# Seven PSUM banks in one tile, waits per bank, any unit in any bank, and a new order of work

## The chip, the cores and the metric

The kernel runs on one core of a Trainium2 chip. The metric is the device time of one launch in microseconds (us). Five engines work side by side on the core, each through its own queue in program order: TensorE (PE) multiplies matrices into PSUM, VectorE (DVE) and ScalarE (ACT) read PSUM and write SBUF, GpSimd (POOL) works from SBUF to SBUF, and SyncE (SP) issues most of the DMAs. PSUM holds eight banks; one bank takes 128 partitions of 512 float32 values, which is the output of one matmul.

## What is computed

The reference mixes two branches, row by row, with a gate:

```
g = sigmoid((x * gate_w).sum(-1))                 # x: 2048 x 448
a = softmax(q k^T / sqrt(28)) v, 16 heads, @ wo    # q, k, v = x @ wqkv
b = irfft2(rfft2(B_x) * (w_r + 1j w_i))            # 2048 x 448
out = g * a + (1 - g) * b
```

In the data as given `B_x` plays no part: the reference hands `x = A_x` to both branches. All inputs and the output are bfloat16.

## The kernel before

**Tiling of the attention.** The sixteen heads form four groups `g` of four heads `s`; the 2048 queries form four blocks `c` of 512. The sixteen pairs (g, c) are numbered `n` and run one after the other. For each n the 2048 keys are sixteen tiles `kt` of 128. A *unit* (n, kt, s) is one matmul of 32 rows of `k` by 512 columns of `q`; its output is one PSUM bank of 128 keys by 512 queries. The four heads of a tile use four different groups of 32 rows of the PE array, so up to four units can run side by side; PE work of this kind is called *row* work below. The sums over the keys (`pv`, four matmuls of 32 output columns each), the projections and most of the Fourier branch use four groups of 32 columns instead, which is *column* work.

**Two ways to take the exponential.** For most tiles ACT reads two units at once, 128x1024, and writes `exp` into a ring of 28 slots (`ring`, L1034). There are 374 such steps. For 69 tiles, given by `ND` and called d tiles, DVE takes an approximate exponential instead: one `tensor_scalar` a unit (L993) writes 16-bit patterns into `pd`, and three `int64_add` of POOL (L1003) make three shifted copies of them; the four versions are weighted and summed by `pv`.

**The other work.** The Fourier branch (`fwd`, `fwd2`, `mid`, `inv`), the projections of later groups, the normalisation after each n and the output tiles fill the time between. Each piece takes one PSUM bank, named an `Item`, from its first matmul to the DVE or ACT instruction that reads it last.

**PSUM.** `alloc` (L334 to L337) makes separate tiles: `psA` and `psB` with two banks each for the units of ACT, `pvb` with one bank for the sums, and three single banks `bg`. Step i writes `psA` for even i and `psB` for odd i, and so waits for step i-2 of ACT. All else, the units of the d tiles too, goes through the three `bg` banks. The framework derives waits from the tiles that an instruction touches.

**The order.** Nothing is ordered at run time. `Sched.op` collects 3639 operations; `TABLE` holds a list of numbers, found by a search beforehand, in which they are emitted (`Sched.run`), and a list of banks for the Items. Six of the numbers stand for short filler matmuls with zeros (`filler`). Every engine does its share of the list in that order. `step` operations emit both units of a step in one operation.

**The shared port.** `pin` and `ported` make POOL wait for the DVE instructions marked `lk=True`, which work from SBUF to SBUF in 16-bit types, before it goes on to its next instruction.

Of the kernel before, what the change touches and what calls it, by code (L numbers as in the profile page):

```python
# [29 lines left out]
UNITS = 128.0  # L30
# [8 lines left out]
    "eNoN1mNjWEsUQNHxnMG5SW2ltm3bNtPUtm3btm3bto3UdvveX9hf1jakJbHEkXCCJDqJQWKSWCQ2iUPikngkPiEkAUlIEpHEJAkJI0lJMpKc"  # L39
    "UJKCZCApSU6SiniSmuQijHQlQAKiCScZSRoiSXaSlkQlitQk6Ugmkp7UILVINZKNZCG5SVUSheQhWUkOUodkJiVJKRKNlCa1SV5SloSQUFKO"  # L40
    "1Cf5SH5SgBQiBUkxUp6UIRVJYVKEFCXFySZSgWwmlUgJ0oq0JVvIVrKStCPbyHayiqwmVcgOsoZMJGtJZTKJTCZTyFSyjqwnG0g3YpVXG8l0"
    "MoPMJLOIU7PJHDKX7CTziCDzySy/gCwkcWk8Gp8uIovJDL+ELCUJaEK6jKDaRRLRnqQxWU5WkECFqMQ0Ck1Co9JoNDqNQcNoTBqLxqZx6G6y"
    "h+wl+0ioak6iqqfkGXlOXpCXJILcIQ3IfhJJ7pID5B55RV6TKOo+eUMekI7kIXlEHpNo6iCJrqaRGKouOUSS0mQ0pupEYqnkNAU9TJ6Qt2SD"
    "j63ekfckjvpA4qp4qhc5Qo6SlDS+akGOkan0I/lEptHPpAlJoBKq6fQLSaS+Qip6nCRWJ0hqmkR9gxk0TH0lp8hpkoau8WnpGXKWJFX1SG9y"
    "jpwnF8hMepEkU61JOnqJXCZXyFVyjSRX18kNcpOkULfIbZKeplRlaAaakZ4kmWhinoSnUj+hLE2t0qhYvByNzcvTXxCNz/XpVFpVgX6H6Dy9"
    "oqYiHUQyqIzqG0nGm5HvJAaPyX+Qn6Qp+UUyqT+QWf2DSjSLyqo6k+okDk/OK9OGpArtSDvRuDwhX+ezqc60C82uEvD1PhEP439IUp5D/SX/"
    "CKGUMrrac9qV5lSCSqqoprkU0Kw0G81Oc9DcKif9TXLR3NRQS/PQPCovzUdTcEfzKk/z05keaUDj83wqhBagmWlBWogWpkVofpWFhtJ4vCgt"
    "RtuTNqQ47U4LqIw8E+9BS9Ke1PJCyhhtHC+oCqv0vIjiJgMvTaUppoqqtLy4siYlr0p70RKqGi2pqtNSKh0vrVJzYXrTUlSZYaSMKkHT8Bq0"
    "Jk3FmSmrsvFyipi/UF5l5dn5SFpB5eGjaEU1mlZSeXkOPobWopVVB/IbqqiqKhcfS535AdVUTg6mNq2ucvMaqh7tQurTBjQfr0NrKm9qqc+u"
    "MC/DG9J4Bk1dWlsV4XVUDNOI1FUFeEJTkNdTCUwjmpnXV1l4WV6IJzHFeQlegefnFXkDFcs0VDFNXFOTN1KNVWNandfg8U0TVZQnMk1VMhOY"  # L50
# [12 lines left out]
    "6h+om7yaf6j6mt7mPb3C39K7fKCpbx6pW/yxOs3P8idqmhllnqqrfDi5xO/xZ2qcGW/e0RfquXrCL/OyfqIp55/ya3y0eakiVRPfwLxSTf0Y"
    "81rd5s38ZPNGhfs7/AV/q5r7l/ydivAzTDFf3JfwJX0p38K/V/PNB9WflPaRfJB5xT+qT2q2iefL+Bv8DL/OJ5np5rP6ogabIeQRf8af88J+"
    "gvmqvqnH/Av/yhubsaaIf8inmO/qh+JMsE/8p/qlPvOpRjLFNBtK3vJ3/D3/rf6omWaO+av+8n98sVloiP7AP/J/SorlZpYhYoihWgmm+5Hh"
    "huvXfK5ZYRaZN/w3L+qFpuIPlzqnz+V/8G+8oVda6wXmO8/th5lGfpmJKn5y0L+40UvMPPM/SMLqbn6p8drpaMIK1N39SpOE9fA9fS8PLLro"
    "7QO9yYSxpGyECdGhOoZIxvr47aaxj6qFiKKTMycOmW2Gieg6mtYiVHgRQ4OIIraY3SamiCVi6h1mp6nuY+lAxNYJxFGTUMTRIWK/SSJQ1PBx"
    "dZjYZ/aYeDq+TqDjiaEmvqjla/s6vq6v51eZ1SaRSCzq+7giqWjgy/uEerOZ7deYRHqUH+3H+LE+sR7nx/sJfq+ZQE6aOT6JDtNpxFbT0ifV"
    "yXRynVa08W19O9/exxEXTAff0Y80KXRKvc7U9J38QdPKf6Cp9Ef6iaYTqXUanVwcM+nFZ5pWp9OpRGyRXp8xJ8xh84WmFhl0Rl1I7DKFRV/f"
    "z6cQ030ykUmfNwdMZp1FZ9U5RUqRS3T2XXwGsdYcN9l0PnHKZNcD/EA/yGcU+cVgP8Tn0Dl1EXHEFBWnTSaRS2cVQ/1Zk1vHYHl0NnHOxGTD"  # L70
    "fD6dV180XX1mEYtlEbFZft3f3zIFdEEdh2UXf+h685fmEHlEIb3BFNYlxT9aStwx5UURTVgFQVleUVQ/N7lFaXHJFNNTfHE91d8zZcRDU0KX"
    "1DXEffPAlNI1RWldQBQU70w8VkaXFa19OXHbxGfFxHBfVidgI3xCVk1UFIlYdVFOV9Dl9RNTQnyjE/1I/9J8pxV1FVFJ/6A/aRU9yVfWTQVj"
    "03xV8Ys+Mq9NNV1c1Bdf6TNTVTcQv+ld89hU1zV0LVFbTPZPTU0dwmrpSiLSGNZMWPbFvDDzfG093y/wdfRCX1fU0+lZBpaRZWJ1tWOhLAqL"
    "yj6YuOyjWeQvm/o6GsvMGosGuol4axrphnoEaShasEainqgsWrJWrDVrwxKztqwda8+ysSO+sc7OOrAlfqPJwXKyXOyKaaKb6twsD8vLOrJO"
    "rDM75LuwrqwbS8G6s2Z6kz/oo7PNfosP159Nc11H9GBb/Suzzb8xrUSEbqFbi/fmk2mlW+o2Ih9rLvKzr6YAO+ALsraiEIvCC7PWuggryrqK"
    "Nrqt/vf/jKZk10w7vd2318Qu9t1EwIqxVCxceCbsN9NBdxZdRGC9bSc66gixw3fSRz23V/0Vv9S3F501s6lZF91CtBTL/E3fVS/3K7y0g8RK"
    "v8p30zv9Lr/bG5uVdddRbA89WPQUe3xH0VP3EunYft9La7vX7/OdhLLIFrJFrIPoo3vrAWIxW8IGir56Keun++shwtm1bKgAO0BfNWlZP7GO"
    "pWEDdX9h7XgxQQzSg/V6toEN0RtZNDuYXfPdxTA9VN8wQ9hQNlKM0MPEcB3dHvbXzU3TQ4wSw9hwFsOOECP1WDFOXPaj9Gh93Y9ko9gYPVrc"
    "8HFtHzGajWFj9Rjx3YxlP8wtf9vf8Xf9MX/cT9D3/Dg9Xo9nJ/xXN4FNZLFsX9aPDRcn/UQ9iZ3yvcVk1p9F+km6r/jnx7Epeor4Y0awAWwK"
    "m6wHsjg2tg2xy9kKtpKtYoPYVD1Nz9Cv/G8T1aKNaafrqeyBX82ysKliGpupQ208O0vPEMVZCTZTlGSlWGlWhpVl5dhEMVu/8DtZebaLReXL"  # L80
    "WAX208zRFdkmVolVZnP1braHzWB7WRVWlVVj83R1lszOZvf9dDaHLdBr2DQxXcxlr/18PY8t1DNZcruPzRLzGcFFegHLYJfozHax3sxS2GV6"
    "qY5vF4tU9peZLbawBHaJ2MYe+kd+hV4o0trlepGYxR77rWyeWKlX6b/mia/BarKL7BK7zCaLWqw2q8Oe+rrsCqvH6rMGbI3ewZ751bohmyO2"
    "s0Zsrb7KGrNrrAkbTZqy66wZC2fN2Tp9gB1kh9gNFsFuslvsMDvCbrP1+g67yzbo+eIoO8Y26ePsBNuoT7I+bLM+xU6zM6w3u8fOsnPsPLvP"
    "zvgHbIs+7Qval/6X36oXiLP+ITvnz/tterteKi6w7PaNnyso/vbI09kduhdbJlaJ1DaL/et36g1il+7JEtrdOpdNb1eLC/6iv+TXiOd+rdij"
    "U9q8dp8eT1aIjWKd2Kv36/2sgH3r3/n14r3fLg7oD/6gzmQz2t3ijz+kc9jDOredJI7ojz4G7hBbRRq7XETDbSI6bhEMOR7Vm8UecUwLlKgw"
    "nx1Ljuv8NgquFCf0IZHTHhbZ7Cl9Um8Sx8RpndXmscdFIXtR7BS7xBl9Vj9iUfGcLm0vifO6rP3kjwiNKfCCvqgT2fK2kt0vjopL+ry4IB6z"
# [1384 lines left out]
```

## Time and profile before

| | us |
|---|---|
| device time, median of three runs | 380.19 |
| the three runs | 379.89, 380.19, 381.33 |
| span of the profiled execution, first to last instruction | 379.2 |
| PE busy in it | 371.3 |
| ACT busy in it | 351.1 |
| DVE busy in it | 339.1 |
| POOL busy in it | 234.4 |

The profile is of one execution, on the only core. Busy time is the union of an engine's instructions as recorded. Consecutive instructions of one engine overlap in the records, so that a mean duration is longer than the step from one instruction to the next, and a busy PE is not necessarily PE at its peak. For what an instruction costs its engine, the step from one start to the next is read. The clock granted to TensorE was 1.000 of full speed.

### The profile page before, as it was taken

How to read it: one execution, taken by the hardware profiler on the slowest of the kernel's cores; microseconds unless marked ns; L12 is line 12 of the kernel's file. 1: busy time of each engine (PE TensorE's matmuls, PEld its weight loads, DVE VectorE, ACT ScalarE, POOL GpSimd, SP SyncE). 2: the span in 40 equal slices, each digit the busy share in tenths (PEclk: the TensorE clock that was granted, in tenths of full speed). 3: DMA queues.
4: the chain of work that ended last, by engine and by line, in shares of the span. 5: the costliest groups of instructions: out<-in, count | busy, mean ns of one | idle time of the engine just before them, and what ended most of it. 6: DMA issues, size and time to landing. Idle time of an engine off the chain costs nothing.

```text
span 379.2 us, 12643 instructions
## 1 busy us (share of the span) xinstructions
PE 371.3 (98%) x5117; PEld 142.4 (38%) x5117; DVE 339.1 (89%) x665; ACT 351.1 (93%) x389; POOL 234.4 (62%) x264
## 2 busy tenths in 40 slices
PE   8999999999999999999999999999999999999996
PEld 6634223342433333234333434233333323433564
DVE  1768899999999999999999999999999999988744
ACT  2799999999999999999999999999999999999841
POOL 4446465866778866565553565778597778483510
PEclk9999999999999999999999999999999999999999
DMA  6511101010210112211322212223222122222132
GB/s 145 157 34 44 29 18 36 4 36 2 41 52 22 44 41 54 55 38 30 68 60 93 69 40 49 57 61 70 45 64 74 30 69 72 86 64 72 35 103 75
DMA packets 31158, 21.23 MB, mean 56 GB/s; under 512 B 16260, under 2 KB 29052, under 8 KB 31100
## 3 DMA queue, kind: packets, MB, share of 16 engines
q1 hardware_dynamic: 29708, 19.96, 20.7%
q8 instruction: 40, 0.66, 0.7%
q10 hardware_dynamic: 1392, 0.46, 0.5%
q14 instruction: 18, 0.15, 0.1%
HBM read 14.51 MB, written 1.96 MB: 43 GB/s over the span
## 4 chain that ended last, share of the span: by engine, by line
PE 55%; ACT 31%; issue 6%; DVE 4%; DMA 2%; POOL 1%; SPq 0%; DVEq 0%; ACTq 0%; POOLq 0%
ACT ring L1034 31%; PE bg L432 24%; PE pvb L432 17%; PE psA L432 7%; PE psB L432 6%; DVE pd L993 2%; PE bg L435 1%; DMA CS<-cCS 1%; DVE X L1419 1%; POOL pd L1003 1%; DMA Wg<-in_B_w_i_dram 0%; DVE X L1298 0%; DVE q L1178 0%; DVE t L1362 0%; DVE wpq L1224 0%
## 5 line engine op out<-in xcount | busy, mean ns | idle before, releaser
L1003 POOL INT64_ADD pd<-pd x207 | 211.9, 1038 | 96.7 <-DVE pd L993 27.4
L1034 ACT ACTIVATE ring<-psA 128x1024 bf16<-128x1024 f32 x187 | 201.7, 1078 | 4.7 <-PE psA L432 3.2
L1034 ACT ACTIVATE ring<-psB 128x1024 bf16<-128x1024 f32 x187 | 201.7, 1079 | 2.6 <-PE psA L432 1.4
L993 DVE TENSOR_SCALAR pd<-bg 128x512 uint16<-128x512 f32 x276 | 180.9, 681 | 8.5 <-PE bg L432 3.5
L432 PE MATMUL pvb<-pd,vd 128*32 128x512 bf16 x1104 | 96.9, 384 | 0.1
L432 PE MATMUL bg<-q,k 32*128 32x512 bf16 x276 | 96.3, 383 | 0.2
L432 PEld LDWEIGHTS <-k 32*128 32x128 bf16 x1024 | 40.1, 91 | 122.4 <-issue 117.7
L432 PE MATMUL psB<-q,k 32*128 32x512 bf16 x374 | 73.2, 383 | 1.3 <-ACT ring L1034 0.7
L432 PE MATMUL psA<-q,k 32*128 32x512 bf16 x374 | 72.8, 383 | 0.5 <-ACT ring L1034 0.2
L432 PE MATMUL pvb<-ring,vw 128*32 128x512 bf16 x748 | 67.9, 384 | 0.0
L432 PEld LDWEIGHTS <-vd 128*32 128x32 bf16 x1104 | 25.3, 94 | 35.5 <-issue 31.1
L432 PEld LDWEIGHTS <-vw 128*32 128x32 bf16 x748 | 17.5, 94 | 22.7 <-issue 20.5
L432 PEld LDWEIGHTS <-xT 128*128 128x128 bf16 (+5 forms) x512 | 20.3, 97 | 10.7 <-issue 9.7
L432 PE MATMUL bg<-xT,wpq 128*32 128x512 bf16 (+3 forms) x244 | 21.2, 383 | 0.1
L1362 DVE TENSOR_TENSOR t<-bg,Wg 128x450 bf16<-128x450 f32 x32 | 18.8, 614 | 0.6 <-DMA Wg<-in_B_w_i_dram 0.4
L432 PE MATMUL bg<-xT,wpk 128*32 128x512 bf16 (+2 forms) x240 | 18.9, 383 | 0.0
L432 PE MATMUL bg<-wvr,xT 128*128 128x112 bf16 (+2 forms) x192 | 13.7, 213 | 0.0
L1178 DVE TENSOR_TENSOR q<-pvs,Rb 128x512 bf16<-128x512 f32 x15 | 10.9, 729 | 2.6 <-DMA Rb<-rsc 2.6
L1298 DVE TENSOR_TENSOR X<-bg,oc 128x226 bf16<-128x226 f32 (+1 forms) x32 | 12.3, 386 | 0.5
L432 PEld LDWEIGHTS <-CS 128*32 128x32 bf16 x384 | 9.0, 95 | 9.9 <-issue 5.6
L432 PE MATMUL bg<-xtok,CS 128*32 128x225 bf16 (+1 forms) x192 | 11.2, 294 | 0.7 <-DMA CS<-cCS 0.7
L742 DVE TENSOR_SCALAR k<-bg 128x512 bf16<-128x512 f32 x15 | 10.3, 685 | 1.3 <-PE bg L432 1.1
(117 smaller groups left out, 315.4 us busy)
## 6 DMA issues: line engine op xcount, KB each, us to landing
Rb<-rsc SPq DMA_DIRECT2D x60, 64.0 KB
CS<-cCS SPq DMA_DIRECT2D x16, 192.0 KB
V<-xtok SPq DMA_DIRECT2D x16, 113.0 KB
Wg<-in_B_w_i_dram SPq DMA_DIRECT2D x64, 28.1 KB
xtok<-Ab SPq DMA_DIRECT2D x16, 112.5 KB
xtok<-in_A_x_dram SPq DMA_DIRECT2D x3, 448.0 KB
Wg<-in_B_w_r_dram SPq DMA_DIRECT2D x32, 28.1 KB
out_dram<-wpq SPq DMA_DIRECT2D x6, 112.0 KB
```

Source lines behind the costliest of these rows:

```text
L432: self.pin(self.nc.tensor.matmul(out, lhsT=lhsT, rhs=rhs, start=start, stop=stop, **kw))
L435: self.pin(self.nc.tensor.transpose(out=out, in_=in_, identity=self.c("ident")[0:n, 0:n]))
L742: self.pin(nc.vector.tensor_scalar(out=dst, in0=self.bgi(it), scalar1=SQ, scalar2=None, op0=ALU.mult))
L993: self.pin(nc.vector.tensor_scalar(out=ys[:, s, :].bitcast(U16), in0=self.bgi(it), scalar1=127 * UNITS, scalar2=0.0, op0=ALU.add, op1=ALU. ...
L1003: self.pin(nc.gpsimd.int64_add(out=fl(pds), in0=fl(ys), in1=PHASE[f] * 0x0001000100010001))
L1034: self.pin(nc.scalar.activation(out=self.ring[:, u0:u0 + len(st), :], in_=slot[:, 0:len(st), :], func=ACT.Exp, scale=LN2 / UNITS))
L1178: e = self.dve(dv(512), lambda: self.pin(nc.vector.tensor_tensor(out=dst, in0=pvs[:], in1=self.Rb[:], op=ALU.mult)), ds, kk, lk=True)
L1298: self.pin(nc.vector.tensor_tensor(out=free_dims(self.X1[:, t, :], [[F, 2], [-1 if dif else 1, n]], (F - 1) * dif), in0=free_dims(self.bgi ...
L1362: self.pin(nc.vector.tensor_tensor(out=out[:], in0=self.bgi(it)[:, 0:F2].rearrange("p (a f) -> p a f", a=2), in1=free_dims(Wg[:], [[F, 2], ...
L1419: self.pin(nc.vector.tensor_tensor(out=free_dims(self.zt[0:FN], [[128, 4], [1, 128]], 512 * t), in0=self.bgi(it)[0:FN, :].rearrange("p (a ...
```

## The change

All seven banks beside `pvb` become one tile `ps`, and every Item, the units of ACT's steps and of the d tiles among them, can have any bank of it. A step of ACT needs two banks that lie side by side; its two units are two operations of their own now, which may stand anywhere in PE's list, in either order. DVE may convert two units of a d tile in one instruction where `PARTS` says so and their banks lie side by side. Since one tile would make every instruction wait for the last users of any of its banks, `pin` declares for each instruction that it doesn't depend on instructions that use other banks, except on those that the operation names itself and the one before it on its engine. The order and the banks come from a new search, whose table now has four parts: the order, the banks, the widths of ACT's steps and the choice of `PARTS` for each d tile. In the prologue, ACT's copy of a transposed block follows the first exponential (which loads the table), and the transposes are chained.

```diff
-    return np.frombuffer(raw[0], np.uint16).tolist(), np.frombuffer(raw[1], np.uint8).tolist()
+    return [np.frombuffer(r, t).tolist() for r, t in zip(raw, (np.uint16, np.uint8, np.uint8, np.uint8))]
...
+    PARTS = (((0,), (1,), (2,), (3,)), ((0, 1), (2, 3)), ((0, 2), (1, 3)), ((0, 3), (1, 2)),
+             ((0, 1), (2,), (3,)), ((0, 2), (1,), (3,)), ((0, 3), (1,), (2,)),
+             ((0,), (1, 2), (3,)), ((0,), (1, 3), (2,)), ((0,), (1,), (2, 3)))
...
+        if self.sc.used:
+            used = frozenset(self.sc.used)
+            keep = [p for p, u in self.sc.need() if not used & u]
+            if ins.ins.engine in self.before:
+                keep.append(self.before[ins.ins.engine])
+            for other in self.bank_sets:
+                if not used & other:
+                    self.tc.declare_no_dep(ins.ins, group="bank" + repr(sorted(other)), reason="other banks",
+                                           keep=[k for k in keep if k.name in self.bank_sets[other]])
...
-        self.psA = ps.tile([P, 2, 512], F32, name="psA")
-        self.psB = ps.tile([P, 2, 512], F32, name="psB")
+        self.ps = ps.tile([P, 7, 512], F32, name="ps")
         self.pv = ps.tile([P, 512], F32, name="pvb")
-        self.bgt = [ps.tile([P, 512], F32, name=f"bg{i}") for i in range(3)]
...
-            w = 2
+        for w in self.sc.widths:
             self.steps.append(seq[i:i + w])
...
-            for s in range(4):
-                it = Item()
+            for part in self.PARTS[sc.parts[di]]:
+                its, ms = [], []
+                for s in part:
+                    it = Item()
...
+                    self.pin(nc.vector.tensor_scalar(
+                        out=free_dims(ys[:], [[512 * e, w], [1, 512]], 512 * part[0]).bitcast(U16),
+                        in0=self.ps[:, bs[0]:bs[0] + w, :],
+                        scalar1=127 * UNITS, scalar2=0.0, op0=ALU.add, op1=ALU.max))
...
-            slot = self.psA if i % 2 == 0 else self.psB
-            deps = [exps[i - 2]] if i >= 2 else []
...
-            m = sc.op("PE", 0.23, fm, deps, -1000 + i * .001, 0.0, "row", name="score")
+                m = sc.op("PE", 0.22, fm, self.kev[g, kt // 4] + self.qev[g, c], 0.0, 0.0, "row", it, name="score")
...
+                self.pin(nc.scalar.activation(out=self.ring[:, u0:u0 + len(st), :],
+                                              in_=self.ps[:, bs[0]:bs[0] + len(st), :],
                                               func=ACT.Exp, scale=LN2 / UNITS))
```

Decoded, the new table holds 374 widths, all of them 2, and 69 choices of `PARTS`, of which 57 are four single units and 12 have one pair and two singles. It has no filler. Which tiles go to DVE (`ND`) is as before.

More of the change, by code (lines that the diff above doesn't have):

```diff
@@ L254, in __init__ @@
         self.step = self.n = None
-        self.after = []
+        self.after, self.made = [], []
         self.lk = eng == "POOL"
@@ L266, in __init__, with need @@
         self.ops, self.ctx, self.cnt = [], "", {}
+        self.codes, self.banks, self.widths, self.parts = unpack(TABLE)
+        self.used = set()
+    def need(self):
+        return [p for d in self.op_now.deps for p in d.made]
     def op(self, eng, dur, emit, deps=(), key=0.0, rel=0.0, mode=None, acq=None, free=None, lat=None, name=""):
@@ L300, in __init__ @@
         self.port = self.cur = None
+        self.bank_sets, self.before = {}, {}
     def pin(self, ins):
@@ L463, in plan_steps @@
                 u += self.RING - u % self.RING
-            for e, unit in enumerate(st):
+            for unit in st:
                 self.unit_step[unit] = k
@@ L557, in prologue @@
                            (warm,), K0 + i * .01, dur=0.175, acq=None if i else hw, free=hw if i == 19 else None)
-        h3 = Item()
-        homes = [lambda: self.pv[:], lambda: self.psA[:, 0, :], lambda: self.psB[:, 0, :], lambda: self.bgi(h3)]
+        hs = [None, Item(), Item(), Item()]
+        homes = [lambda: self.pv[:]] + [lambda h=h: self.bgi(h) for h in hs[1:]]
         trs, self.xev = [], {}
@@ L577, in fe @@
                     self.pin(nc.vector.tensor_copy(out=self.xT[0][0:n, c, :], in_=src))
-            self.xev[0, c] = sc.op(eng, 0.36 if eng == "DVE" else 0.65, fe, trs[-4:], K0 + 11 + c, name="xev", free=h3 if c == 3 else None)
+            self.xev[0, c] = sc.op(eng, 0.36 if eng == "DVE" else 0.65, fe, trs[-4:] + ([tl] if eng == "ACT" else []), K0 + 11 + c, name="xev", free=hs[c])
         self.kev, self.qev = {}, {}
@@ L584, in prologue @@
             b1 = (lambda i1=i1: self.bgi(i1)) if wi else (lambda: self.pv[:])
-            b2 = (self.psB if wi else self.psA)[:, 0, :]
+            i2 = Item()
+            b2 = lambda i2=i2: self.bgi(i2)
             first = {}
@@ L612, in fe @@
             def fe(b2=b2, dst=dst):
-                self.pin(nc.vector.tensor_scalar(out=dst[:, 0:512], in0=b2, scalar1=SQ, scalar2=None, op0=ALU.mult))
-            (self.kev if w == "k" else self.qev)[0, 0] = [self.dve(0.61, fe, (m,), K0 + 50 + wi)]
+                self.pin(nc.vector.tensor_scalar(out=dst[:, 0:512], in0=b2(), scalar1=SQ, scalar2=None, op0=ALU.mult))
+            (self.kev if w == "k" else self.qev)[0, 0] = [self.dve(0.61, fe, (m,), K0 + 50 + wi, free=i2)]
     def weights(self):
@@ L677, in bgi @@
     def bgi(self, item, dt=F32):
-        t = self.bgt[item.bank][:]
+        t = self.ps[:, item.bank, :]
+        self.sc.used.add(item.bank)
         return t if dt == F32 else t.bitcast(dt)
@@ L1031, in attention, with fe @@
             u0, ug = self.unit_slot[st[0]]
-            def fe(st=st, slot=slot, u0=u0):
-                self.pin(nc.scalar.activation(out=self.ring[:, u0:u0 + len(st), :], in_=slot[:, 0:len(st), :],
+            def fe(st=st, u0=u0):
+                us = sorted(st, key=lambda u: uit[u].bank)
+                bs = [uit[u].bank for u in us]
+                assert all(b == bs[0] + j for j, b in enumerate(bs))
+                self.sc.used.update(bs)
+                for u, slot in zip(us, sorted(self.unit_slot[u] for u in us)):
+                    self.unit_slot[u] = slot
+                self.pin(nc.scalar.activation(out=self.ring[:, u0:u0 + len(st), :],
+                                              in_=self.ps[:, bs[0]:bs[0] + len(st), :],
@@ L1035, in fe @@
                                               func=ACT.Exp, scale=LN2 / UNITS))
-            e = self.act(0.052 + 512 * len(st) / 1200.0, fe, [m] + exps[-1:], i * .001, name="exp")
-            e.step = i
+            e = self.act(0.052 + 512 * len(st) / 1200.0, fe, ms + exps[-1:], i * .001, name="exp", free=[uit[u] for u in st])
+            e.step, e.unit0 = i, st[0]
             e.n = [self.unit_slot[u][1] for u in st]
@@ L1104, in attention @@
             if o.name == "score":
-                for u in self.steps[o.step]:
-                    kr[self.groups[u[0]][0]].append(o)
+                kr[self.groups[o.n[0]][0]].append(o)
         for m in self.dunit_ops:
@@ L1232, in last_tile @@
         i = t - 12
-        it = Item() if i > 1 else None
-        bank = lambda: (self.psA[:, 0, :] if i == 0 else self.psB[:, 0, :] if i == 1 else self.bgi(it))[:, 0:D]
-        ops = [self.lastexp[i]] if i < 2 else []
+        it = Item()
+        bank = lambda: self.bgi(it)[:, 0:D]
+        ops = []
         for k in range(8):
```

273 lines of the change are left out of this document (142 added, 131 removed).

## Prediction

> **What bounds the kernel now.** I read the page first: its busy line, its slices and its chain of waits.
>
> ```profile
> span 379.2 us, 12643 instructions
> PE 371.3 (98%) x5117; PEld 142.4 (38%) x5117; DVE 339.1 (89%) x665; ACT 351.1 (93%) x389; POOL 234.4 (62%) x264
> ...
> PE   8999999999999999999999999999999999999996
> ...
> DVE  1768899999999999999999999999999999988744
> ACT  2799999999999999999999999999999999999841
> ...
> PE 55%; ACT 31%; issue 6%; DVE 4%; DMA 2%; POOL 1%; SPq 0%; DVEq 0%; ACTq 0%; POOLq 0%
> ```
>
> Three engines are full nearly all the time, and the chain that ended last runs through PE for 55% and ACT for 31%. So I ask the table of windows where each of them has room.
>
> ```profile
> 100.00:120.00 20.00, 19.55 (x274) 7.57 (x271) 19.59 (x42) 20.00 (x23) 13.92 (x15) 1.00 0.15 42
> 160.00:180.00 20.00, 20.00 (x283) 7.96 (x287) 19.64 (x39) 19.12 (x22) 11.37 (x12) 1.00 0.14 32
> 180.00:200.00 20.00, 20.00 (x305) 7.03 (x307) 19.31 (x39) 18.40 (x21) 10.72 (x12) 1.00 0.26 63
> 260.00:280.00 20.00, 19.57 (x243) 6.66 (x243) 19.85 (x40) 20.00 (x23) 14.95 (x16) 1.00 0.26 56
> ```
>
> The columns after the window's length are the busy times of PE, PEld, DVE, ACT and POOL. The kernel changes its bound as it goes: at 100 to 120 and 260 to 280 ACT has no idle time and PE has a little; at 160 to 200 PE has none and ACT loses 0.88 + 1.60. DVE is never far off: 0.15 to 0.69 idle in 20.
>
> How much does ACT lose in all? Its timeline has the first step, a stretch without a gap, a late one and the last:
>
> ```profile
> 12.74 1.02 ACT L1034 ACTIVATE ring<-psA 128x1024 bf16<-128x1024 f32 x1 [0.31 <-PE psB L432]
> ...
> 41.61 1.05 ACT L1034 ACTIVATE ring<-psA 128x1024 bf16<-128x1024 f32 x1
> 42.51 1.06 ACT L1034 ACTIVATE ring<-psB 128x1024 bf16<-128x1024 f32 x1
> 43.42 1.07 ACT L1034 ACTIVATE ring<-psA 128x1024 bf16<-128x1024 f32 x1
> 44.32 1.08 ACT L1034 ACTIVATE ring<-psB 128x1024 bf16<-128x1024 f32 x1
> ...
> 364.96 1.02 ACT L1034 ACTIVATE ring<-psB 128x1024 bf16<-128x1024 f32 x1
> ```
>
> A step takes (44.32 - 41.61) / 3 = 0.903. The 374 steps start between 12.74 and 364.96, 352.2 apart; 373 steps without a gap would be 373 x 0.903 = 336.8. So 15.4 are lost between steps, some to small instructions of ACT, most to units that come late. The long waits, in brackets, lie at the start, around 160 to 200 and at the end, and PE ends them:
>
> ```profile
> 16.40 1.02 ACT L1034 ACTIVATE ring<-psB 128x1024 bf16<-128x1024 f32 x1 [0.81 <-PE psA L432]
> ...
> 194.95 1.02 ACT L1034 ACTIVATE ring<-psA 128x1024 bf16<-128x1024 f32 x1 [0.62 <-PE psA L432]
> ...
> 361.50 1.02 ACT L1034 ACTIVATE ring<-psA 128x1024 bf16<-128x1024 f32 x1 [0.69 <-PE psA L432]
> ```
>
> The 15.4 are the most the middle of the kernel can give: ACT's floor is 379.2 - 15.4 = 363.8 as long as the ends stay (12.74 before the first step, 14.2 after the last one's start).
>
> PE's own price list I take from its timeline.
>
> ```profile
> 149.95 0.37 PE L432 MATMUL bg<-X,A 128*32 128x450 bf16 x4
> 150.15 0.39 PE L432 MATMUL pvb<-pd,vd 128*32 128x512 bf16 x4
> 150.47 0.39 PE L432 MATMUL psB<-q,k 32*128 32x512 bf16 x2
> 150.48 0.39 PE L432 MATMUL bg<-q,k 32*128 32x512 bf16 x1
> 150.79 0.40 PE L432 MATMUL pvb<-pd,vd 128*32 128x512 bf16 x4
> 151.02 0.57 PE L432 MATMUL bg<-Bd,xT 128*32 128x226 bf16 x16
> ...
> 153.28 0.39 PE L432 MATMUL psA<-q,k 32*128 32x512 bf16 x2
> 153.60 0.40 PE L432 MATMUL pvb<-pd,vd 128*32 128x512 bf16 x4
> 153.83 0.39 PE L432 MATMUL bg<-xT,wpq 128*32 128x512 bf16 x4
> ```
>
> A column pass of 512 followed by column work takes 0.23 (150.79 to 151.02, 153.60 to 153.83). Followed by row work it takes 0.32 (150.15 to 150.47). A row pass before column work takes 0.32, with three units (150.47 to 150.79) as with two (153.28 to 153.60). So a change between row and column work costs about 0.09, a row pass itself 0.23, and a *visit* to row work, one pass and two changes, 0.32 + 0.32 - 0.23 = 0.41, however many of the four heads share it.
>
> **The change, part by part.**
>
> *What ACT and the matmuls do* stays: 374 steps of 128x1024, the same units and sums, the same tiles on DVE.
>
> *PE's list.* I read both tables as data, operation by operation. The old list goes to row work 358 times with 382 passes, the new one 347 times with 371 passes: eleven visits fewer, 11 x 0.41 = 4.5. Counted in stretches of 34 steps, seven of the eleven lie in the first, fifth, sixth and eleventh stretch, which is where ACT waits for units today: by the number of steps (34 take 31 or more, from 12.74) these are the start, some 60 before 201, and the end; four lie where ACT has no idle time, and there time saved on PE buys nothing. So 7 x 0.41 = **2.9** counts; bounds 0 and 4.5.
>
> *The fillers.*
>
> ```profile
> L432 PE MATMUL pvb<-zero 128*32 128x256 bf16 (+2 forms) x24 | 1.1, 257 | 0.0
> ```
>
> Six filler operations go, 1.1 of PE at most. They stood where the old order kept PE busy on purpose, so some of it may have been idle anyway: **0.6**, bounds 0 and 1.1.
>
> *The pool of banks.* Today the units of a step wait for the step two before, whatever else is free. In the old list two pairs of units are issued ahead of a step's own place at 62 of 374 steps, in the new one two or more at 192. That covers small delays, not work that is missing. Of the 15.4 I take the eleven visits and fillers to settle 3.5; of the other 11.9 a deeper lead could win anything from 0 to 11.9. I take **1.5**, near the lower end: in the PE-bound windows the work is what is late, and DVE, with 0.36 and 0.69 idle there, can't follow much faster.
>
> *Waits per bank.* A unit now waits for the last reader of its own bank, ACT or DVE. Queued behind a waiting unit is all of PE: column passes, and with them DVE, ACT and the chain of sums. Cost 0 if the planned times hold; the other end is the slower rival below.
>
> *More signals.* The two units of a step are two operations that needn't be neighbours. The rows above bound it: three units for two readers take 0.32, two units for one reader 0.32; to the last digit shown a signal costs 0 to 0.01, for 374 more of them 0 to 3.7. I take 0.
>
> *Wide conversions.*
>
> ```profile
> L993 DVE TENSOR_SCALAR pd<-bg 128x512 uint16<-128x512 f32 x276 | 180.9, 681 | 8.5 <-PE bg L432 3.5
> L704 DVE COPY xT<-bg 128x1024 bf16<-128x1024 bf16 x3 | 2.0, 681 | 0.2 <-PE bg L435 0.2
> ```
>
> Twelve pairs become 12 instructions of 1024: 264 in place of 276. No such form is in the trace; it lies between 0.68 (the copy of 1024 from 16-bit) and 2 x 0.68, so DVE gains 0 to 12 x 0.68 = 8.2. The operand is float32, so I take the upper end, near 0. It delays the first of the two banks; DVE isn't what ends the chain (4%), so 0 on the path either way.
>
> *The shared port.*
>
> ```profile
> 83.43 1.04 POOL L1003 INT64_ADD pd<-pd  x1 [0.45 <-DVE sq L747]
> ...
> 83.78 0.71 DVE L905 CAST gg<-ge 128x16 bf16<-128x16 f32 x1
> ...
> 86.30 0.41 DVE L747 TENSOR_TENSOR sq<-q 128x512 bf16<-128x512 bf16 x1
> ...
> L747 DVE TENSOR_TENSOR sq<-q 128x512 bf16<-128x512 bf16 x15 | 6.3, 433 | 0.0
> ...
> L903 DVE TENSOR_SCALAR ge<-ge 128x16 f32<-128x16 f32 x1 | 0.2, 165 | 0.0
> ```
>
> A small cast takes 0.71 where its neighbour takes 0.165: it ends with POOL's addition, 0.55 late. An order that reckons with such holds can save them, but there is little to save: a square that isn't held takes 0.41, the mean of its fifteen is 0.433, so all fifteen lost 15 x 0.023 = 0.35. With the cast, and as much for each of the four other kinds that work from SBUF to SBUF, an estimate of 0.55 + 5 x 0.35 = 2.3 is the upper bound and 0 the lower, all on DVE; 0 on the path, since DVE has 4% of the chain.
>
> *Ends.* Before the first step the list holds 74 operations of PE in place of 73, after the last 65 in place of 64 (eight sums in place of four, three output operations fewer). Each is a pass of 0.2, one way and the other: 0, bounds -0.8 and +0.8.
>
> **Sum.** 2.9 + 0.6 + 1.5 = 5.0. Span 379.2 - 5.0 = 374.2. The runs stand 1.0 above the span (380.19 - 379.2), taken as unchanged: **375.2**, 1.3% less than the median. With the bounds of the list, the fillers and the lead together, 380.2 - 4.5 - 1.1 - 11.9 = 362.7, which ACT's floor cuts to 364.8; at the other end 380.2 + 3.7 + 0.8 = 384.7. About 0.5%, or 1.9, is what a measurement of this kernel can tell from no change: 378.3 to 382.1 is "same".
>
> **The rivals.**
>
> *1. Three full engines (same, 379.4; chance 0.16).* PE gets its eleven visits, but DVE is the next bound: with 0.15 to 0.69 idle in 20, a stretch can shrink by some 2% at most before DVE is late, and a late DVE holds the banks. For it: the DVE column of the windows. Against it: the busy time of DVE is a union of records that overlap, so there is more room than it shows. Only the start gives something, two visits, 0.8: 379.4.
>
> *2. Late DVE holds up ACT (slower, 383.5; chance 0.10).* Today a late conversion can only delay a `bg` bank; ACT's units have banks of their own. In the pool a unit may get a bank that DVE reads last. PE runs in order, so one late release stops the row pass with the next step's units in it. Price: a hold as in the cast above, 0.55, passed on. It decides once it happens more than 5.0 / 0.55 = 9 times on the path; at 15 times it is +3.3. For it: DVE's small slack. Against: a lead of two pairs absorbs 0.9.
>
> *3. Signals (same, 378.9; chance 0.04).* Every unit signals its own end, 0.01 each: 375.2 + 3.7. The rows allow it, but show no sign of it. The Trainium skill's page "TensorE: Matmul & The Clock Gate", in "The cost: per-tile semaphore tail", puts 26.3 ns on each increment; for 374 more that would be 9.8, an estimate, and 385.0 in all. By that rule three units with two signals should take longer than two with one; the trace, with 0.32 for both, doesn't agree.
>
> *4. Waits aren't per bank after all (far slower; chance 0.02).* If the declarations failed, each unit would wait for the last reader of any bank, that is for the step just issued: a step of 1.02, then a row pass of 0.39, in turn: 1.41 in place of 0.903, 374 x 0.51 = 190 more, 570. PE's idle time would show it at once.
>
> *5. Both floors nearly met (faster, 369; chance 0.13).* The lead wins most of the 11.9: 380.2 - 3.5 - 8. For it: ACT would be at its floor of 0.903 nearly all the time, and POOL at 62% is no hindrance. Against: the PE-bound windows, where PE has no idle time to give.
>
> *Forecast (370.5 to 378.2, likeliest 375.2; chance 0.55).*
>
> **How the numbers follow.** Faster by over 0.5%: 0.55 + 0.13 and little else, 0.68. Same: rivals 1 and 3, 0.20. Slower: rivals 2 and 4, 0.12. The range runs from rival 5, 369, to just under rival 2, 382.5; it leaves out about 0.1 on either side. The forecast's own range is 370.5 to 378.2.
>
> **What would show it.** Right: the first step of ACT near 12.7 and the last near 360, the lost time between steps down from 15.4 to about 10; ACT's idle time at 160 to 200 of before smaller by half; a row visit of three or four units still 0.41. Rival 1: ACT's loss as before, with DVE at 19.9 in the windows. Rival 2: PE idle before units, ended by DVE's conversions. Rival 3: row passes of 0.33 or more. What would make the forecast wrong: row passes that break in two because a bank is late, so that the 371 passes of the list become 400 or more on the chip; and a longer tail after the last step.

## The result, and where the time went

| | median, us | runs | span of the profile | granted clock |
|---|---|---|---|---|
| before | 380.49 | 379.89 to 381.33 | 379.2 | 1.000 |
| after | 390.03 | 389.91 to 390.39 | 388.3 | 0.991 |

The change made the kernel slower: the ratio is 1.0245, with a 95% interval of 1.0226 to 1.0264. The forecast was 375.2, its range 369.0 to 382.5.

The page of the changed kernel answers to the first lines of before: span, busy times, slices and the chain of waits by engine.

```profile
span 388.3 us, 12544 instructions
PE 373.4 (96%) x5093; PEld 141.7 (36%) x5093; DVE 338.7 (87%) x653; ACT 351.9 (91%) x389; POOL 234.5 (60%) x264
...
ACT  2799999999999999999989999999999959999731
...
PEclk9999999999999999999999999999999969999999
...
PE 70%; DVE 10%; ACT 9%; DMA 5%; issue 3%; POOL 1%; SPq 1%; DVEq 0%; ACTq 0%; POOLq 0%
```

The busy times of DVE and ACT hardly moved (339.1 to 338.7, 351.1 to 351.9). PE's grew by 2.1 (371.3 to 373.4), some of it at a lower clock, and its idle time by 7.0 (379.2 - 371.3 = 7.9 to 388.3 - 373.4 = 14.9). Two rows of slices have a mark that before lacks: ACT has a 5 late in the kernel, and the clock has a 6 in the same slice. DMA's share of the chain went from 2% to 5%. ACT's timeline of after says when:

```profile
12.53 1.94 ACT L1074 ACTIVATE ring<-ps 128x1024 bf16<-128x1024 f32 x2 [0.21 <-PE ps L463]
...
310.78 1.02 ACT L1074 ACTIVATE ring<-ps 128x1024 bf16<-128x1024 f32 x1 [0.15 <-PE ps L463]
313.70 1.02 ACT L1074 ACTIVATE ring<-ps 128x1024 bf16<-128x1024 f32 x1 [1.90 <-PE ps L463]
...
371.27 1.95 ACT L1074 ACTIVATE ring<-ps 128x1024 bf16<-128x1024 f32 x2
```

From the first step's start to the last one's end it is 371.27 + 1.95 - 12.53 = 360.7; before it was 364.96 + 1.02 - 12.74 = 353.2. So 7.5 went between the steps, 388.3 - 373.2 = 15.1 in place of 379.2 - 366.0 = 13.2 is spent behind them (1.9), and the head is 0.2 shorter: together 9.2, and the spans differ by 9.1. Step by step, the two kernels are level within 0.2 up to step 170 (171.7 and 171.9); the new one is 0.9 behind at step 187, 2.3 at step 221, 3.3 from step 238 to step 306, 7.8 at step 323, and then no more. Most of the loss sits at three places in the middle, and at the end. Another 0.5 goes around step 196, at 199; what stops PE there was not followed up.

What stops PE there? The waits of PE that a semaphore ended, first of after and then of before (total, count, longest):

```profile
PE ps L463 <- DMA CS<-cCS: 2.8, 3, 1.5
...
PE pvb L463 <- DVE rr L1184: 1.3, 1, 1.3
PE ps L463 <- DVE vt L904: 1.1, 1, 1.1
```

```profile
PE bg L432 <- DMA CS<-cCS: 0.7, 1, 0.7
```

*The largest place, 306 to 323.* PE's timeline of after, with the wait in brackets:

```profile
309.75 0.57 PE L463 MATMUL ps<-xtok,CS 128*32 128x450 bf16 x12 [0.52 <-DMA CS<-cCS]
...
312.69 0.37 PE L463 MATMUL ps<-xtok,CS 128*32 128x450 bf16 x4 [1.50 <-DMA CS<-cCS]
312.99 0.61 PE L463 MATMUL ps<-q,k 32*128 32x512 bf16 x2
```

PE stands before the spectral matmuls of groups 14 and 15, whose constants `CS` have not come. Behind the second wait a row pass takes 0.61, not 0.39: the clock is at half there. Why is `CS` late? SP's issues, of after and of before:

```profile
304.76 0.55 SPq L438 DMA_DIRECT2D Wg<-in_B_w_r_dram  x1
305.35 0.57 SPq L438 DMA_DIRECT2D wpq<-in_A_wo_dram  x1
305.97 0.55 SPq L438 DMA_DIRECT2D Wg<-in_B_w_r_dram  x1
306.62 0.53 SPq L438 DMA_DIRECT2D Rb<-rsc  x1
307.25 0.37 SPq L438 DMA_DIRECT2D CS<-cCS  x1
...
309.34 1.19 SPq L438 DMA_DIRECT2D CS<-cCS  x1
```

```profile
301.95 0.33 SPq L407 DMA_DIRECT2D CS<-cCS  x1
302.32 0.55 SPq L407 DMA_DIRECT2D Wg<-in_B_w_i_dram  x1
302.91 0.58 SPq L407 DMA_DIRECT2D CS<-cCS  x1
```

Read the first column against the duration: each issue starts when the one before ends. SP waits for nothing; it is busy issuing, mostly about 0.55 each (the last `CS` issue takes 1.19, for which the trace names no reason), and the two loads stand behind the rest. The last matmuls on the two old tiles ended at 303.4 and 305.2, so the buffers were free while SP issued `Wg`, `Wpq` and `Rb`. From issue to the end of PE's wait it is 309.75 - 307.25 = 2.5 and 312.69 - 309.34 = 3.4. In before the loads were issued at 302 and 303, 4.0 and 4.9 ahead of their use, and the first had nothing to spare: PE's one wait for `CS`, 0.72, is there, at 305.9.

*220.* The same, for group 4 (SP, PE and DVE of after):

```profile
217.79 0.98 SPq L438 DMA_DIRECT2D CS<-cCS  x2
...
220.48 0.57 PE L463 MATMUL ps<-xtok,CS 128*32 128x450 bf16 x12 [0.80 <-DMA CS<-cCS]
222.11 1.16 DVE L1400 TENSOR_TENSOR t<-ps,Wg 128x450 bf16<-128x450 f32 x2 [1.93 <-DMA Wg<-in_B_w_r_dram]
```

*177.* DVE's timeline of after, and under it POOL's. Two of DVE's operations that work from SBUF to SBUF take 1.11 and 1.52 while POOL's additions run (the first `Z` of the rows, also beside an addition, isn't held); the evictions queue behind them, and PE waits 1.1 for the bank of `vt`:

```profile
172.82 0.27 DVE L1407 TENSOR_TENSOR Z<-t 128x225 bf16<-128x225 bf16 x1
173.00 1.11 DVE L1405 TENSOR_TENSOR Z<-t 128x225 bf16<-128x225 bf16 x1
...
174.37 1.52 DVE L1216 TENSOR_TENSOR q<-pvs,Rb 128x512 bf16<-128x512 f32 x1
```

```profile
170.86 4.49 POOL L1038 INT64_ADD pd<-pd  x4
```

*The end.* A conversion of DVE waits 2.78 for an output transfer to leave its buffer, the reciprocal stands behind it, and PE waits for the reciprocal:

```profile
379.04 0.71 DVE L1262 TENSOR_SCALAR wpk<-ps,glog 128x448 bf16<-128x448 f32 x1 [2.78 <-DMA out_dram<-wpk]
379.65 0.24 DVE L1184 RECIPROCAL rr<-pvb 128x16 f32<-128x16 f32 x1
```

### The profile page after: what moved, and what is told of

It is laid out like the page before. It is cut to its first block, busy times and chain, and to the rows that moved or that the text cites. A ratio compares the mean times of both kernels' runs of the same rounds, so it can differ in the third digit from the quotient of the medians.

```text
span 388.3 us, 12544 instructions
## 1 busy us (share of the span) xinstructions
PE 373.4 (96%) x5093; PEld 141.7 (36%) x5093; DVE 338.7 (87%) x653; ACT 351.9 (91%) x389; POOL 234.5 (60%) x264
## 4 chain that ended last, share of the span: by engine, by line
PE 70%; DVE 10%; ACT 9%; DMA 5%; issue 3%; POOL 1%; SPq 1%; DVEq 0%; ACTq 0%; POOLq 0%
PE ps L463 45%; PE pvb L463 24%; ACT ring L1074 9%; DVE pd L1024 4%; DMA CS<-cCS 2%; DMA Rb<-rsc 1%; PE ps L466 1%; SPq L438 1%; DVE X L1336 1%; DVE q L1216 1%; DMA out_dram<-wpk 1%; POOL pd L1038 1%; DVE pvs L1204 1%; DMA rsc<-rr 0%; DMA wpk<-in_A_wo_dram 0%
## 5 line engine op out<-in xcount | busy, mean ns | idle before, releaser
L1074 ACT ACTIVATE ring<-ps 128x1024 bf16<-128x1024 f32 x374 | 346.8, 1072 | 13.6 <-PE ps L463 13.2
L1024 DVE TENSOR_SCALAR pd<-ps 128x512 uint16<-128x512 f32 (+1 forms) x264 | 179.1, 707 | 11.1 <-PE ps L463 8.3
L463 PE MATMUL ps<-q,k 32*128 32x512 bf16 x1024 | 147.9, 386 | 2.6 <-ACT ring L1074 1.6
L1400 DVE TENSOR_TENSOR t<-ps,Wg 128x450 bf16<-128x450 f32 x32 | 18.9, 617 | 4.4 <-PE ps L463 2.1
L463 PE MATMUL ps<-xT,wpq 128*32 128x512 bf16 (+3 forms) x248 | 20.1, 383 | 0.6 <-DVE wpq L553 0.3
L463 PE MATMUL ps<-xT,wpk 128*32 128x512 bf16 (+3 forms) x244 | 19.7, 384 | 0.2 <-DVE k L767 0.2
L463 PE MATMUL ps<-wvr,xT 128*128 128x112 bf16 (+2 forms) x192 | 13.4, 213 | 1.2 <-DVE vt L904 1.1
L463 PEld LDWEIGHTS <-CS 128*32 128x32 bf16 x384 | 8.9, 96 | 15.2 <-issue 7.9
L463 PE MATMUL ps<-xtok,CS 128*32 128x225 bf16 (+1 forms) x192 | 10.9, 300 | 3.0 <-DMA CS<-cCS 2.8
L1336 DVE TENSOR_TENSOR X<-ps,oc 128x226 bf16<-128x226 f32 (+1 forms) x32 | 12.2, 384 | 0.5
L463 PE MATMUL ps<-wpk,q 128*32 128x448 bf16 x128 | 11.6, 362 | 0.0
```

The lines of the kernel that those rows point to most:

```text
L463: self.pin(self.nc.tensor.matmul(out, lhsT=lhsT, rhs=rhs, start=start, stop=stop, **kw))
L1024: self.pin(nc.vector.tensor_scalar(out=free_dims(ys[:], [[512 * e, w], [1, 512]], 512 * part[0]).bitcast(U16), in0=self.ps[:, bs[0]:bs[0] ...
L1074: self.pin(nc.scalar.activation(out=self.ring[:, u0:u0 + len(st), :], in_=self.ps[:, bs[0]:bs[0] + len(st), :], func=ACT.Exp, scale=LN2 / ...
L1336: self.pin(nc.vector.tensor_tensor(out=free_dims(self.X1[:, t, :], [[F, 2], [-1 if dif else 1, n]], (F - 1) * dif), in0=free_dims(self.bgi ...
L1400: self.pin(nc.vector.tensor_tensor(out=out[:], in0=self.bgi(it)[:, 0:F2].rearrange("p (a f) -> p a f", a=2), in1=free_dims(Wg[:], [[F, 2], ...
```

## The experiments

The theory that I formed from these lines: the loss is in the order, at four places where a queue of its own (SP's, or DVE's) was late, and not in the banks or the form of the code. The rivals were the prediction's own: signals, wide conversions, waits that aren't per bank.

**Form or order?** The old order and the old banks, written as a table for the new form: one tile, declared waits, each unit an operation.

```diff
-codes, banks = the new table
+codes = the old table, each score split in its two units
+banks = psA -> 0 and 1, psB -> 2 and 3, bg b -> 4 + b
```

> The old order and the old banks (two pairs for ACT, three single banks, six fillers) written in the new form: one tile of seven banks, waits declared per bank, units of a step as two operations next to each other. Theory A (the loss is in the new order): the form costs nothing, 380.5, between 378.6 and 382.4. Theory B (the form itself costs: one tile, waits per bank, signals of single units): a large part of the 9.5 is still there, 384 to 390.

Measured: 381.42 beside 381.00 for before, ratio 1.0008 (0.9994 to 1.0022), span 379.0. The form costs nothing that can be measured, and the traces say why: the two programs are nearly the same. Both have 12643 instructions and 955 matmuls that update a semaphore, so two units that stand side by side in the list still share one signal. The run therefore doesn't test more signals; the changed kernel has 1018 such matmuls, 63 more. What was lost came with the new order and its banks.

**Wide conversions.** The twelve pairs back to single units, all else as after.

```diff
-PARTS choice of 12 d tiles: one pair and two singles
+PARTS choice of 12 d tiles: four singles
```

> The new kernel with the twelve conversions of 1024 undone, each as two of 512 at the same place. Theory A: 390.0, within 0.8. If the wide conversions hold two banks too long: 388 or less.

Measured: 391.83, ratio to before 1.0269 (1.0223 to 1.0315), 1.8 above after's median, where 0.8 had been allowed: a miss in size. Three of its executions, at a mean clock of 0.986 to 0.991, took 391.6 to 392.3, one at 1.000 took 388.43. None came near before, so the wide conversions aren't the cause. What they cost themselves, from the groups of after by form:

```profile
L1024 DVE TENSOR_SCALAR pd<-ps 128x512 uint16<-128x512 f32 x252 | 165.6, 682 | 10.5 <-PE ps L463 8.0 <-PE pvb L463 0.8
L1024 DVE TENSOR_SCALAR pd<-ps 128x1024 uint16<-128x1024 f32 x12 | 14.6, 1218 | 0.5 <-PE ps L463 0.3
```

One of 1024 takes 1.22, two of 512 take 2 x 0.68 = 1.36; but neighbours overlap (in the rows of 177, `Z` of 0.27 at 172.82 is followed at 173.00), so little is won.

**Loads early, by the list.** Each `CS` load put right behind the operation that frees its buffer.

```diff
 PE mid(g-2)#5: last matmul on the old CS
+SP mid(g)#0: CS load
...
-SP mid(g)#0: CS load
```

> The new kernel with one thing changed in its list: each load of CS for g of 2 and more is issued right behind the matmul that frees its buffer. Theory A, with late loads as its largest part: PE's waits for CS at 220, 310 and 313 go, and with them the half clock from 313 to 319; 390.0 - 4.4 - 0.9 = 384.7, between 383.0 and 386.5. Theory B: 390, since the waits for CS are then only a place where lost time shows.

Measured: 441.72, ratio 1.1599 (1.1559 to 1.164). A miss, and an instructive one. SP's own waits:

```profile
SPq L436 <- PE ps L461: 110.2, 20, 18.1
```

The list is one order for all engines, but each runs through its part at its own pace. SP runs ahead; a load that stands where PE's operation stands makes SP wait for it, up to 18.1, with every later issue behind it. Places in SP's list have to be chosen by time.

**Loads early, by the trace.** SP's order changed at two places, so that each load is issued just after its buffer comes free.

```diff
 SP q<-nrow (213.0)
+SP Wg(4) #5, Wg(4) #1, CS(5), CS(4)
 SP Wg(5) x5
-SP Wg(4) #5, CS(4), CS(5), Wg(4) #1
...
+SP CS(15)
 SP rsc, Wg(14)
+SP CS(14)
 SP wpq, Wg(15), Rb
-SP CS(14)
 SP Wg(15), Rb, wpq
-SP CS(15)
```

> The changed kernel, with only SP's order of issues altered at two places, by the times of its own profile: CS of spectral groups 4 and 5 and two tiles of Wg ahead of the five Wg loads that stood before them (CS(4) issued near 215.6 instead of 217.79), and CS(15) and CS(14) in front of the Wpq and Rb loads (near 304 and 305.5 instead of 309.34 and 307.25). Theory L (late loads behind SP's issues of 0.55 us are the largest loss): the waits of TensorE for CS at 220.5 (0.80), 309.8 (0.52) and 312.7 (1.50) go, the stretch at half clock from 313 to 319.5 with them, and the exponentials from step 306 to step 323 take 15.4 to 16.5 us instead of 19.9: 385.0 +-1.0. Theory P (TensorE's queue is late there for other reasons, the loads are only the last of several waits): 389 to 390.5, another wait at the same places.

Measured: 384.26 (382.06 to 384.84), ratio 1.0069 (1.004 to 1.0097): by the medians 5.8 of the 9.5 are back, by the ratios 1.8 of 2.4 per cent. From step 306 to step 323 it takes 15.6, where after took 20.7. The windows of its profile, first where after had waited (columns: window, its length, busy time of PE, PEld, DVE, ACT, POOL, then granted clock, DMA share, GB/s), then behind the wait of 1.1 at 177, which was left in:

```profile
309.00:313.00 4.00, 4.00 (x66) 1.39 (x59) 4.00 (x8) 4.00 (x6) 4.00 (x4) 1.00 0.27 80
313.00:316.00 3.00, 3.00 (x51) 0.96 (x43) 2.95 (x10) 3.00 (x5) 1.27 (x3) 1.00 0.02 3
...
176.00:179.00 3.00, 1.92 (x25) 1.19 (x24) 3.00 (x6) 2.14 (x3) 0.00 (x0) 0.97 0.11 31
179.00:182.00 3.00, 3.00 (x25) 0.49 (x22) 2.03 (x6) 2.24 (x3) 2.05 (x2) 0.50 0.19 56
```

The same stretch in after, for comparison:

```profile
309.00:313.00 4.00, 1.98 (x32) 0.56 (x29) 3.03 (x6) 2.65 (x3) 3.75 (x4) 1.00 0.44 128
313.00:316.00 3.00, 3.00 (x32) 0.67 (x28) 1.25 (x2) 1.86 (x2) 0.33 (x1) 0.50 0.01 1
316.00:319.50 3.50, 3.50 (x32) 0.69 (x28) 1.97 (x6) 2.09 (x3) 0.78 (x1) 0.50 0.00 0
```

The half clock is gone where the wait is gone, and in this profile it follows the wait at 177 instead. The two parts of the loss can be told apart: e4_no_pairs and e6_tail2 have both waits for `CS` at 310 and 313 (0.68 and 1.19, 0.53 and 1.65) but no half clock there, and take 17.6 and 17.9 from step 306 to step 323. Of the 5.1 between 20.7 and 15.6 the half clock is thus about 3, the waits about 2.

**The pair alone.** Only CS(15) and CS(14) moved, as in the second half of that diff.

> The changed kernel, with only CS(15) and CS(14) moved in front of the Wpq and Rb loads near 304 to 305 us; nothing altered near 213 to 220. If this pair is the larger part of what e5_loads won (5.8): 385.6 +-0.8, the waits at 220.5 and 222.1 as before. If the first place carried it: 388 to 389.

Measured: 387.44 (386.67 to 388.45), ratio 1.0173 (1.0146 to 1.02), less than hoped. Its steps from 306 to 323 take 15.6 too, 5.1 less than in after. The profile shows where that was given back: step 17 starts 0.8 later than in after (PE waits 1.7 for the input at the start), and the tail behind the last step is 385.8 - 368.6 = 17.2 long, 2.1 more. There the conversion waits 3.29 for an output transfer (DVE's timeline), PE is busy 1.24 of the 3.0 from 374 to 377, and the clock drops again (0.80 in this window, 0.63 in the next 3.0). Nothing in the edit bears on the start.

```profile
374.95 0.71 DVE L1260 TENSOR_SCALAR wpk<-ps,glog 128x448 bf16<-128x448 f32 x1 [3.29 <-DMA out_dram<-wpk]
```

**The same fault in the old order.** In e1_old_order, two loads moved back in SP's order.

```diff
-SP CS(14), Wg(14), CS(15), Rb, Rb, Wg(15), Wg(15)
+SP Wg(14), Rb, Rb, Wg(15), Wg(15), CS(14), CS(15)
```

> The old order in the new form (e1_old_order, 381.4) with one thing made worse in SP's order: the CS loads of groups 14 and 15 stand behind three Wg loads and two Rb loads that followed them, so that CS(14) is issued near 305.8 instead of 302.3. Theory L (a load late behind SP's issues stops TensorE, whatever the order): TensorE waits about 2.8 for CS near 306 and the time is 384.2, up to 387 if a stretch at half clock follows the wait. Rival (the old order's lead absorbs a late load): 381.4 +-0.8.

Measured: 385.12 (384.36 to 386.14), ratio 1.0113 (1.009 to 1.0137), 3.7 above e1_old_order. PE's waits have one of 3.0, and the windows show PE idle from 305 and the clock behind it:

```profile
PE ps L458 <- DMA CS<-cCS: 3.2, 2, 3.0
```

```profile
305.00:308.40 3.40, 0.38 (x11) 0.08 (x7) 1.56 (x3) 1.63 (x2) 2.92 (x4) 0.90 0.51 151
308.40:312.00 3.60, 3.60 (x34) 0.90 (x34) 1.13 (x2) 1.71 (x2) 0.39 (x1) 0.50 0.10 19
```

A load late behind SP's issues stops the old order just as it stops the new one. So this part of the loss, the largest, is shown from both sides.

**The tail, twice.** First the reciprocal alone, then the reciprocal and the eviction of group 15 ahead of the conversion that waits.

```diff
-DVE out_tile 11 (wpk), reciprocal 15, X 15
+DVE reciprocal 15, out_tile 11 (wpk), X 15     (first)
+DVE reciprocal 15, X 15, out_tile 11 (wpk)     (second)
```

> The new kernel with the reciprocal of the last normalisation moved ahead of the conversion of output tile 11 in DVE's list, two neighbours swapped. If the wait of 1.34 on PE at 379.9 is on the path: 390.0 - 1.4 = 388.6, between 388.0 and 389.2. If the output DMAs end the kernel anyway: 390.0.

Measured: 389.31 (387.57 to 390.57), ratio 1.0218 (1.0182 to 1.0255), tail unchanged. The reciprocal runs at 377.99 now, and the wait moved to the next operation that PE needs, the eviction of `X` behind the same conversion:

```profile
378.95 0.71 DVE L1260 TENSOR_SCALAR wpk<-ps,glog 128x448 bf16<-128x448 f32 x1 [0.70 <-DMA out_dram<-wpk]
379.56 0.68 DVE L1455 TENSOR_TENSOR X<-ps,ogb 113x512 bf16<-113x512 f32 x1
```

> The changed kernel, with both the reciprocal of pair 15 and the inverse transform's eviction of group 15 ahead of out_tile 11's conversion in DVE's order. If the head of DVE's queue is what delays the tail: 388.6 +-0.5, the tail behind the last exponential 14.7 to 15.2 us instead of 16.1. If only the output transfers do: 390.0 +-0.4, tail 16.1, the wait moved once more.

Measured: 387.92 (385.96 to 390.24), ratio 1.02 (1.0141 to 1.0258); from the start of the last step to the end 15.1, where after has 16.1 and 14.7 to 15.2 was expected. Its four runs fall in two pairs: 385.96 and 386.21 with a mean clock of 0.998 and 0.999, 389.64 and 390.24 with 0.991. After's four runs all have 0.991, and 390.1 on average; e6_tail2's two at that clock have 389.9. So the profile shows the 1.0 of the tail, but most of the 2.1 between the medians is the clock.

**The hold.** `Z` and `q` moved behind the three evictions.

```diff
-DVE Z(0), sq, q(4), t(1), vt, t'(1)
+DVE sq, t(1), vt, t'(1), Z(0), q(4)
```

> The changed kernel, with two of DVE's SBUF-only operations at 173 to 176 us (Z of group 0, 1.11 us, and the q product of pair 4, 1.52 us, both of which ran beside GpSimd's additions) moved behind three evictions (mid 1's two and V's). Theory H (the hold on the shared port makes the eviction late for which TensorE waits 1.12 us at 177.0): that wait goes, the two operations take 0.27 and 0.68, step 187 starts 0.8 to 1.1 earlier, 389.0 +-0.4. Rival: TensorE is late there anyway, or it waits for the moved operations next: 389.7 to 390.6.

Measured: 389.47 (387.07 to 391.28), ratio 1.0219 (1.017 to 1.0267), which holds after's 1.0245: alone, not told from no change. The profile shows the mechanism, though. `Z` and `q` run at their own price, and PE's wait for `vt` is gone. The hold has moved: `sq`, now beside POOL's addition, takes 1.26 where it took 0.41 in after.

```profile
174.03 1.26 DVE L770 TENSOR_TENSOR sq<-q 128x512 bf16<-128x512 bf16 x1
...
177.02 0.27 DVE L1403 TENSOR_TENSOR Z<-t 128x225 bf16<-128x225 bf16 x1
177.21 0.68 DVE L1214 TENSOR_TENSOR q<-pvs,Rb 128x512 bf16<-128x512 f32 x1
```

By the distance of the steps less 0.90, one step of after lost 1.06 there; now the next one loses 0.80: most of it was PE's work anyway. So the rival, that PE is late there anyway, holds for the greater part.

**Together**, with and without the hold:

> The three edits of e5_loads, e6_tail2 and e7_port together. If the losses are separate, they add: 382.5 +-1.5, about the time of before or 1 us more. If one hides another: 384.5 to 386.

> e8_all without the edit of e7_port, that is with DVE's two operations held beside GpSimd again. If the hold is worth something of its own: 382.2 to 384.0, the wait of 1.1 at 177 back. If it is worth nothing: 381.9 +-0.4.

Measured: all three edits 381.87 (381.22 to 382.72), ratio 1.0017 (1.0003 to 1.003); without the hold's edit 383.19 (381.92 to 388.25), ratio 1.0058 (1.0039 to 1.0077). The separate gains were 5.8 + 2.1 + 0.6 = 8.5 by the medians, together 8.2. That doesn't prove that they add, since the medians of e6_tail2 and e7_port mix executions with and without a stretch at half clock; together, none of ten has a mean clock under 0.998. Without the edit of the hold the wait at 177 is back, the median is 1.3 higher, and two of ten runs are over 385, at a mean clock of 0.996 and 0.987. By these two the edit is worth little in its own wait, more in what follows the wait.

Of the version with all three: the page, the largest of PE's waits, and the last two steps in ACT's timeline.

```profile
span 379.7 us, 12548 instructions
PE 369.8 (97%) x5093; PEld 141.6 (37%) x5093; DVE 337.3 (89%) x653; ACT 350.8 (92%) x389; POOL 234.3 (62%) x264
```

```profile
PE ps L461 <- ACT ring L1072: 1.6, 6, 0.4
```

```profile
363.94 1.95 ACT L1072 ACTIVATE ring<-ps 128x1024 bf16<-128x1024 f32 x2
```

The longest total among PE's waits is ACT's, 1.6, and no load is among them. The steps, from 12.68, take 363.94 + 1.95 - 12.68 = 353.2, to a tenth what they took before. With the three faults mended the new order is within 0.3% of the old one; no version beat before.

## Why the prediction was wrong

*What bounds the kernel* was read rightly: three engines full, the loss in ACT's waits for PE. It was also the warning: with so little slack a stop of PE is hardly made up. Of the waits of 0.52 and 1.50 and the half clock behind them, 4.5 stayed in the steps.

*The step that failed* is *Waits per bank*, "Cost 0 if the planned times hold", in an account that costed PE's list, DVE's conversions and the banks and had no term for SP. The planned times didn't hold. The new order moves SP's loads too, and not one of the rows that priced the change was an SP row. The rows were there: issues of 0.55 back to back, the loads issued 4.0 and 4.9 ahead of their use, and a wait of 0.7 for `CS` in before already. From these a bound would have followed: a load a few issues later stops PE by about 0.55 for each issue beyond its slack. Measured: 5.8 of 9.5 by the medians, in the two places of e5_loads. About 3 of the 5.1 from step 306 to step 323 was the half clock behind the stop, for which the account had no term either.

*PE's list, 2.9*: the count came true and the price didn't. In the traces 357 visits become 348, and in the four stretches where ACT waits 34, 32, 30 and 28 become 31, 32, 28 and 26, seven fewer as planned. But a visit is not always one pass. Measured from its first unit to the next column pass, a visit takes 0.32 at the median when its units start together, and 0.53 when one of them starts more than 0.1 behind the one before. Such gaps go from 30 in before to 46 in after and 43 in e8_all. All visits between the first and the last step take 124.6 in before and 123.9 in e8_all: nine fewer won 0.7, not 9 x 0.32 = 2.9. Passes that break in two were named as what would make the forecast wrong. Why these units start late, no run tests.

*Fillers, 0.6, and the pool, 1.5.* PE's busy time with the faults mended is 1.5 under before (371.3 to 369.8), up to 1.1 of it the fillers, but the steps take 353.2 as before, so neither term bought anything. No run separates the two.

*Conversions and declared waits at 0* fit e4_no_pairs and e1_old_order, where nothing came back and nothing was lost; e1_old_order has the declared waits with the old order alone. *Signals at 0* was not tested, and its count was wrong: 63 more matmuls update a semaphore, not 374, so the bound worked out from the rows is 63 x 0.01 = 0.6 and not 3.7. The Trainium skill, "TensorE: Matmul & The Clock Gate", "The cost: per-tile semaphore tail", puts 26.3 ns on each increment; for 63 that would be 1.7, an estimate, and no run here shows or excludes it.

*The shared port* was sized from the holds of before and bounded at 2.3. The new order has single holds of 1.11 - 0.27 = 0.84 and 1.52 - 0.68 = 0.84, on the path. Together 1.7, under the bound; but that 0 would reach the path was wrong, at one place, where step 187 stands 0.9 later than in before.

*Ends, 0 with 0.8 either way*: the tail grew by 1.9. Counting PE's passes missed that DVE's queue stood behind an output transfer.

*The rivals.* "Three full engines" has the outcome that remains once the faults are mended, ACT's loss as before, but not its own sign: DVE is busy 19.3 to 19.7 of 20 from 160 to 220 in e8_all, not 19.9, and PE 20.0 from 180 to 200. "Late DVE" has one case in the middle, at 177, not fifteen. None had a load that comes late.

## What to carry to other kernels

When an order is rewritten, compare every queue, SP's first: for each load, when its buffer comes free, when it is issued and when it is used, with the issue time that the trace shows. On a kernel whose main engine is 98% busy, look for the first late semaphore, not for the sum of saved work. A gain counted in a list is a plan; count it again in the trace.

## What I hadn't expected of the hardware

A short stop of PE can cost more than itself. In after, waits of 0.52 and 1.50 left PE 1.98 of 4.0 busy, and the clock was 0.50 for the next 6.8; in e9_old_late 0.38 busy of 3.4 was followed by 0.50, in e5_loads 1.92 of 3.0. It isn't certain to happen: the same wait at 177 left after at a clock of 1.00, and so did the two waits for `CS` in e4_no_pairs and e6_tail2. e6_tail2 has two runs with a mean clock of 0.991 and two with 0.998 and 0.999, 389.9 and 386.1 on average, 3.9 apart; a mean clock of 0.991 says about as much, 0.009 x 388 = 3.5. The Trainium skill, "TensorE: Matmul & The Clock Gate", in "HAM oscillation — how this bites in real kernels", gives as the rule that PE shouldn't stand idle for more than about 3.4 us. The stops named here are shorter, the longest 3.0, so the runs don't agree with it as a limit for one gap.

Where the stop falls decides a good part of it. In every trace the changes of the granted clock lie whole multiples of 3.41 apart: in after at 312.97 and 319.80, in e10_loads_late_pair at 375.80 and 379.21. Here are the pieces of that grid with the two waits for `CS`, first of after, then of e4_no_pairs:

```profile
309.56:312.97 3.41, 1.72 (x27) 0.55 (x27) 2.47 (x5) 2.09 (x3) 3.41 (x4) 1.00 0.41 121
```

```profile
309.27:312.68 3.41, 2.59 (x37) 0.71 (x34) 2.80 (x6) 3.10 (x4) 3.14 (x4) 1.00 0.55 138
312.68:316.09 3.41, 2.37 (x36) 0.76 (x40) 2.20 (x5) 2.04 (x3) 1.84 (x2) 1.00 0.23 73
```

In after both waits fall into one piece, PE is busy for 0.50 of it, and half clock follows. In e4_no_pairs they fall into two pieces (0.76 and 0.70), in e6_tail2 too (0.67 and 0.70), and the clock stays. In the thirteen traces every piece at full clock with PE busy for less than 0.4 was followed by half clock, and none with more than 0.73. Between the two both occur: at 177 a piece of 0.67 was followed by half clock in e5_loads and not in e11_loads_tail.

Nine in ten of SP's 316 issues in after take 0.30 to 0.63, a few more than 1 (up to 1.6), and issues follow each other without overlap; the kernel's own planner allows 0.15. That the planner therefore took the loads to be in time is likely, but wasn't tried.
